# Waiting inside TensorE's own queue where the fill banks change rows, and one dealing of the fills for all slots

## The chip, the cores and the metric

The kernel runs on one core of one Trainium2 chip. A core has five engines that run side by side, each through its own queue in order: TensorE (PE in the profile; its weight loads are listed apart as PEld), VectorE (DVE), ScalarE (ACT), GpSimd (POOL) and SyncE (SP), which issues the transfers. Engines wait for each other through semaphores. The metric is the device time of one execution in microseconds (us). Time before: 720.57 us, the median of 3 runs (719.08 to 722.27).

## What is computed

The input has 2048 tokens of 512 channels. Sliding-window attention with 32 heads of 16 channels (window 256) gives `s`; a channel MLP gives a gate; all is float32.

```python
def reference(A_x, A_wqkv, A_wo, B_x, B_w1, B_b1, B_w2, B_b2):
    x = A_x                                  # (1, 2048, 512)
    xn = _layernorm(x)
    s = _A_ref(xn, A_wqkv, A_wo)             # q, k, v = xn @ wqkv; 32 heads of 16; 0 <= i - j < 256
                                             # softmax(q k^T / 4) v @ wo
    g = _silu(_B_ref(xn, B_w1, B_b1, B_w2, B_b2))
                                             # gelu(layernorm(xn) @ w1 + b1) @ w2 + b2, hidden size 1792
    return x + s * g
```

## The kernel before

**Stages.** First the tokens are normalised and transposed and the first projections are made (steps t = -16 to -1). Then the attention runs over 64 *slot pairs* u = 0 to 63 (128 slots, t = 2u and 2u + 1): eight groups of four heads, and in each group eight pairs of query blocks. From some 403 us on come the MLP, the output projection and the end.

**Fills.** Everything that attention doesn't need at once (the projections of later head groups, the values, and the first hidden rows of the MLP) is cut into single pairs of matmuls, the *fills*, and these are put between the attention's own matmuls. A fill pair uses the array by halves: one matmul on the upper 64 rows of the array, one on the lower 64, side by side, each into a PSUM bank of its own (`fb0`, `fb1`; in the first stage also the banks named `pair`). A job goes through two phases. In phase 0 bank 0 gets the products of one half of the rows and bank 1 those of the other; in phase 1 the banks change rows, so that each bank ends with a whole sum. [...] That is the *turn* of a job. `tandem` (line 505) makes two jobs of 12 pairs (24 for the values) a phase over a span of slots (t0, t1), mostly six slots long; `by_halves` (line 360) does it for the first stage.

**How a turn is secured.** An otherwise useless small write of another engine stands between: it waits for the last pair of phase 0, and the first pair of phase 1 waits for it. This *mark* is a VectorE memset of one column (`fixed[:, 7:8]`), a ScalarE copy or a GpSimd memset, and it stands in that engine's queue between its other work. Where no mark is named, `by_halves` lets the turn wait for VectorE's last masked copy of the attention maxima (`outs["max"]`).

**How the slots are dealt.** A slot pair's work on TensorE is set by the loop at lines 991 to 1034: scores of the exponentials (`prob_part`, into `stb`, read by ScalarE), products for the row maxima (`max_ends` into `xy`, `max_middle` into `zo`, read by VectorE), fills, and the product with the values (`pv_part`, into `zo`, named `zo<-pt,vt` in the profile). `some(todo, first, last)` issues the quarters `first` to `last` of a slot's fills. An ordinary even slot issues one quarter, then the products of `max_middle`, then the other three; an ordinary odd slot issues `early` quarters, `max_middle`, then up to `last`, `max_ends`, and the rest. For spans of six slots (`turned`, all but the spans of the values' later jobs and the last one) the slot t0 + 2 is in `turns`: there all fills of phase 0 are issued ahead of `max_middle`, and in the odd slot after it `early` and `last` are one to two quarters later.

**Order on an engine.** The class `Ordered` keeps each engine's instructions in the order of the program text; no scheduler moves them.

Of the kernel before, what the change touches and what calls it, by code (L numbers as in the profile page):

```python
# [23 lines left out]
NQ = H // 4  # L24
EPS = 1e-5
LEAD = 12
EARLY = 10
ORDER = mybir.DependencyInfo(mybir.DependencyClass.Sync, mybir.DependencyReason.DATA)
# [21 lines left out]
def mixer_kernel(ctx, tc, x, wqk, wv, wo, w1, b1, w2, b2, out):  # L50


    nc = SimpleNamespace(**{name: Ordered(tc, name) for name in ("tensor", "vector", "scalar", "gpsimd", "sync")})
# [131 lines left out]
    ends_of = xy.rearrange("q a (p e k) -> q a p e k", p=2, e=2)  # L185
    psf = attn.enter_context(tc.tile_pool(name="psf", bufs=1, space=PSUM))
    fb = [psf.tile([P, 512], F32, name=f"fb{i}") for i in range(2)]
    early = ExitStack()
# [27 lines left out]
    fixed = const.tile([P, 8], F32, name="fixed")  # L216
    mhalf = fixed[:, 0:4]
# [7 lines left out]
    mask = upper.bitcast(I32).unsqueeze(1).unsqueeze(1).to_broadcast([P, 2, 2, P])  # L225
    b1s = const.tile([P, NF], F32, name="b1s")
    sv = small.tile([P, 32], F32, tag="sv", name="sv", bufs=1)
# [129 lines left out]
            return half, finish, box  # L357
        return [(216, mm, i) for i in range(len(ops))], finish

    def by_halves(job, banks, first, second, seer=None):  # L360

        half, finish, box = job
        box[:] = banks
        seen = []
        for phase, where in enumerate((first, second)):
            for i in range(12):
                flags = dict(start=(phase == 0 and i == 0), stop=(phase == 1 and i == 11), skip_group_check=True)

                def unit(i=i, phase=phase, flags=flags):
                    if phase == 0 and i == 0:  # L370
                        box[:] = [bank() if callable(bank) else bank for bank in box]
                    two = (half(box[1 - phase], 1 - phase, i, slice(64, P), **flags),
                           half(box[phase], phase, i, slice(0, 64), **flags))
                    if phase == 0 and i == 11 and seer:
                        seen.append(seer())
                        for r in two:
                            tc.add_manual_dep(seen[0].ins, r.ins.name, ORDER, reason="the rows are through")
                    if phase == 1 and i == 0:
                        for r in two:
                            tc.add_manual_dep(r.ins, (seen or outs["max"])[0].ins.name, ORDER, reason="the banks change rows")  # L380
                fills.setdefault(where[len(where) * i // 12], []).append((unit, ()))
        fills[second[-1]].append((finish, ()))

# [76 lines left out]
        return t  # L460

    taken = set()
    turns = set()
    todo_dve = []

    def late(fn, *args):
# [38 lines left out]
    def tandem(t0, t1, one, two, mid=None, back=None):  # L505

        n = one[0]
        lo, hi, seen = slice(0, 64), slice(64, P), []
        turned = t1 - t0 == 5 and not back
        mid = mid or (t0 + t1 + 1) // 2  # L510

        def places(slots):
            cuts = [n * k // len(slots) for k in range(len(slots) + 1)]
            return [(t, 0) for t, a, b in zip(slots, cuts, cuts[1:]) for _ in range(b - a)]
        if turned:
            turns.add(t0 + 2)
        first, second = places(range(t0, mid)), places(range(back or mid, t1 + 1))
        for phase, where in enumerate((first, second)):
            for i in range(n):
                flags = dict(start=(phase == 0 and i == 0), stop=(phase == 1 and i == n - 1), skip_group_check=True)  # L520

                def unit(i=i, phase=phase, flags=flags):
                    made = ((two if phase == 0 else one)[1](fb[1 - phase], i, hi, **flags),
                            (one if phase == 0 else two)[1](fb[phase], i, lo, **flags))
                    if phase == 0 and i == n - 1:
                        seen.append(nc.scalar.copy(fixed[:, 6:7], mhalf[:, 0:1]) if t0 < 16 * NQ - LEAD and not turned else
                                    nc.vector.memset(fixed[:, 7:8], 0.0))
                        for r in made:
                            tc.add_manual_dep(seen[0].ins, r.ins.name, ORDER, reason="the rows are through")
                    if phase == 1 and i == 0:  # L530
                        for r in made:
                            tc.add_manual_dep(r.ins, seen[0].ins.name, ORDER, reason="the banks change rows")
                fills.setdefault(where[i], []).append((unit, ()))
        fills.setdefault((t1, 0), []).append((one[2], (fb[0], t1, nc.scalar.copy)))
        if t1 >= 16 * NQ - LEAD:
            fills[t1, 0].append((two[2], (fb[1], t1, nc.vector.tensor_copy)))
        else:
            fills.setdefault((t1, 2), []).append((two[2], (fb[1], t1, nc.scalar.copy)))
# [27 lines left out]
    def max_ends(n, qb):  # L566

        mt, _ = max_places(n, qb)
        for p in range(2):
            for a in (1, 0):  # L570
                if qb == 0:
                    max_scores(ends_of[:, a, p, 0], n, qb, a, p, lambda row: row[:, P * qb: P * qb + 1].to_broadcast([64, P]))
                    max_scores(ends_of[:, a, p, 1], n, qb, a, p, lambda row: row[:, P * qb: P * (qb + 1)])
                else:
                    max_scores(ends_of[:, a, p], n, qb, a, p,
                               lambda row: row.rearrange("d (b k) -> d b k", k=P)[:, max(qb - 2, 0): qb + 1: 2 if qb > 1 else 1])
        own = ends_of[:, :, :, 1]
        outs["max"] = nc.vector.copy_predicated(own, mask, ends_of[:, :, :, 0]),
        return lambda: nc.vector.tensor_reduce(out=mt, in_=own, axis=AX.X, op=ALU.max, negate=True)

    def max_middle(n, qb):
# [259 lines left out]
    def free_bank():  # L841
        return ps_st.tile([P, 512], F32, tag="b", name=f"pair_{now[0]}")

    others = [free_bank, free_bank]
    by_pool, by_dve, by_act = (lambda: nc.gpsimd.memset(sv[:, 31:32], 0.0), lambda: nc.vector.memset(sv[:, 30:31], 0.0),
                               lambda: nc.scalar.copy(sv[:, 29:30], mhalf[:, 0:1]))
    for job, banks, first, second, *seer in (
            (job_qk(0, 2), fb, [(-8, 0)], [(-7, 0)]), (job_v(0, 4), others, [(-8, 0), (-8, 1)], [(-7, 1)], by_dve),
            (job_v(0, 5), fb, [(-5, 0)], [(-5, 1)], by_act), (job_qk(0, 3), others, [(-5, 1)], [(-4, 1)], by_pool),
            (job_v(0, 6), fb, [(-4, 0)], [(-4, 1), (-3, 1)]), (job_v(0, 7), fb, [(-2, 1), (-1, 1)], [(-1, 2)], by_pool),  # L850
            (job_qk(1, 0), others, [(-3, 1)], [(-2, 1)]),
            (job_qk(1, 1), fb, [(0, 0)], [(1, 0)], by_act)):
        by_halves(job, banks, first, second, *seer)
    fills.update(spread([job_x(3)], [(-6, 0), (-6, 1)]))
    fills[-10, 0][:0] = fills[-11, 1][-5:]
    del fills[-11, 1][-5:]
# [129 lines left out]
    def some(todo, first, last):  # L986

        n = sum(fn.__name__ == "unit" for fn, _ in todo)
        for fn, args in todo[-(-n * first // 4): -(-n * last // 4) if last < 4 else len(todo)]:
            fn(*args)  # L990
    for u in range(end // 2):
        t = 2 * u
        prob_part(u, 1)
        rest = own_max(max_ends, t + LEAD)
        calm[0] = t < end - LEAD
        even, odd = (fills.pop((v, 0), []) for v in (t, t + 1))
        now[:] = t, 0
        run(delayed.pop((t, 0), ()))
        early = 4 if t in turns else 1
        some(even, 0, early)  # L1000
        own_max(max_middle, t + LEAD)
        rest()
        planned(t)
        some(even, early, 4)
        fill_in(t, 1)
        ended(t)
        t += 1
        prob_part(u, 2)
        now[:] = t, 0
        run(delayed.pop((t, 0), ()))  # L1010
        early = 2 if u % 8 == 7 else 1
        last = 2 if u % 8 == 0 else 3
        if t - 1 in turns:
            early, last = last, last + 1
        some(odd, 0, early)
        own_max(max_middle, t + LEAD)
        some(odd, early, last)
        planned(t)
        fill_in(t, 1)
        own_max(max_ends, t + LEAD)()  # L1020
        calm[0] = False
        own_rows(t + LEAD, t)
        for fn, args in todo_dve:
            fn(*args)
        todo_dve.clear()
        if u % 8:
            some(odd, last, 4)
        if t + 1 < end:
            prob_part(u + 1, 0)
        if u % 8 == 0:  # L1030
            some(odd, last, 4)
        fill_in(t, 2)
        pv_part(u)
        ended(t)
# [483 lines left out]
```

## Time and profile before

| what | value |
|---|---|
| median of 3 runs | 720.57 us (719.08 to 722.27) |
| the profiled execution's own time | 720.63 us |
| span of the profile | 718.5 us |
| PE busy | 709.2 us (99%) |
| DVE, ACT, POOL busy | 507.9, 409.5, 298.4 us (71, 57, 42%) |
| granted TensorE clock | 0.999 |
| VectorE marks in tile `fixed` | 19, 59 ns each, first at 75.5, last at 394.2 us |
| ScalarE marks in `fixed` and `sv` | 3 of 191 ns, 2 of 192 ns |

Times in the windows and rows are counted from the span's start. A slot pair is measured here from the start of its predecessor's product with the values to the start of its own. Matmuls are pipelined and their ends are modelled, so a busy PE isn't PE at its peak: a stall shows as a later start. In a row of the timeline x8 is a run of eight matmuls, and the time beside the start goes from the first one's start to the last one's end.

### The profile page before, as it was taken

To read this page: it belongs to the slowest core of one execution; us is meant where nothing else is said; L and a number is where in the kernel's file an instruction comes from. 1 tells how busy PE (TensorE), PEld (TensorE's weight loads), DVE (VectorE), ACT (ScalarE), POOL (GpSimd) and SP (SyncE) were. 2 spreads that over 40 slices of the span, in tenths; PEclk is the share of its full clock that TensorE was granted. 3 is DMA by queue.
4 is the path that set the end of the run, shared out by engine and by line. 5 is a ranking of instruction groups with operands and counts; after the bars stand their busy time and mean duration, and the time that the engine had idled before them with its cause. 6 is when DMAs were issued, how large, how long until landed. Compare 5 with 4: busy or idle time off the path is not lost.

```text
span 718.5 us, 17700 instructions
## 1 busy us (share of the span) xinstructions
PE 709.2 (99%) x6912; PEld 573.6 (80%) x6912; DVE 507.9 (71%) x880; ACT 409.5 (57%) x612; POOL 298.4 (42%) x498
## 2 busy tenths in 40 slices
PE   8999999999999999999999999999999999999997
PEld 7998777777778887767777788888888888888886
DVE  6887778878777677788893767346586856767923
ACT  7767777767676676768877735132354644541001
POOL 7344767666576655757777340204203000001102
PEclk9999999999999999999999999999999999999999
DMA  8325366776448876677744658155222312253701
GB/s 298 84 49 117 89 150 147 174 185 140 94 101 255 271 261 199 176 179 201 201 135 136 200 170 290 66 149 202 88 88 89 118 58 88 82 186 120 243 15 59
DMA packets 66274, 106.95 MB, mean 149 GB/s; under 512 B 12624, under 2 KB 21072, under 8 KB 66192
## 3 DMA queue, kind: packets, MB, share of 16 engines
q1 hardware_dynamic: 66192, 105.82, 51.1%
q8 instruction: 55, 0.90, 0.5%
q14 instruction: 27, 0.22, 0.1%
HBM read 54.80 MB, written 33.82 MB: 123 GB/s over the span
## 4 chain that ended last, share of the span: by engine, by line
PE 93%; DVE 2%; ACT 2%; DMA 1%; POOL 1%; issue 1%; SPq 0%; DVEq 0%; ACTq 0%; POOLq 0%
PE acc L42 21%; PE fb L42 21%; PE zo L42 15%; PE p L42 9%; PE stb L42 7%; PE s L42 6%; PE h L42 6%; PE xy L42 6%; PE pv L42 2%; ACT pt L42 1%; DVE mt L42 1%; DMA x<-in_x_dram 1%; DMA w<-w_d 0%; DVE xy L42 0%; PE tr L42 0%
## 5 line engine op out<-in xcount | busy, mean ns | idle before, releaser
L42 ACT ACTIVATE pt<-stb 128x1024 f32<-128x1024 f32 (+1 forms) x176 | 177.6, 1009 | 49.6 <-PE stb L42 42.5
L42 POOL TENSOR_SCALAR_AFFINE_SELECT pt<-pt 128x512 f32<-128x512 f32 (+1 forms) x296 | 163.7, 573 | 73.7 <-ACT pt L42 70.1
L42 DVE COPY_PREDICATED xy<-upper,xy 128x512 f32<-128x512 int32 x128 | 88.9, 694 | 37.2 <-PE xy L42 34.9
L42 PE MATMUL fb<-xnT,wqb 64*128 64x512 f32 (+2 forms) x732 | 114.0, 390 | 0.5 <-DVE xy L42 0.2
L42 POOL TENSOR_TENSOR xo<-xo,gated 128x512 f32<-128x512 f32 x15 | 19.9, 1329 | 221.5 <-DVE gated L42 220.5
L42 PE MATMUL acc<-w,gh 128*128 128x512 f32 x320 | 98.6, 389 | 0.0
L42 PE MATMUL zo<-pt,vt 128*17 128x128 f32 (+1 forms) x1920 | 90.5, 327 | 0.8 <-DVE mt L42 0.6
L42 DVE TENSOR_REDUCE mt<-xy 128x4 f32<-128x512 f32 x128 | 88.0, 688 | 2.9 <-DVE xy L42 0.6
L42 DVE TENSOR_REDUCE mt<-zo 128x4 f32<-128x512 f32 x120 | 82.8, 690 | 9.8 <-PE zo L42 7.5
L42 PE MATMUL stb<-qk 64*128 64x384 f32 (+1 forms) x704 | 77.8, 298 | 1.5 <-ACT pt L42 1.0
L42 PEld LDWEIGHTS zo<-pt,vt 128*17 128x17 f32 x1920 | 50.3, 97 | 33.5 <-POOL pjr L42 2.6
L42 PEld LDWEIGHTS stb<-qk 64*128 64x128 f32 x704 | 54.9, 185 | 22.3 <-ACT pt L42 12.5
L42 PEld LDWEIGHTS acc<-w,gh 128*128 128x128 f32 x320 | 60.1, 188 | 12.5
L42 PEld LDWEIGHTS fb<-xnT,wqb 64*128 64x128 f32 (+1 forms) x732 | 62.4, 186 | 5.3 <-DVE fixed L42 0.5
L42 PE MATMUL acc<-w,gl 128*128 128x512 f32 x160 | 62.3, 389 | 0.0
L42 PE MATMUL xy<-qk 64*128 64x256 f32 (+2 forms) x576 | 62.2, 298 | 0.0
L42 PEld LDWEIGHTS xy<-qk 64*128 64x128 f32 x576 | 45.3, 186 | 8.7 <-DVE mt L42 4.2
L42 PE MATMUL p<-xnT 128*128 128x512 f32 x189 | 51.8, 389 | 0.0
L42 PEld LDWEIGHTS zo<-qk 64*128 64x128 f32 x480 | 39.7, 185 | 10.7 <-DVE mt L42 6.4
L42 PE MATMUL s<-wos,ohl 128*128 128x512 f32 (+1 forms) x204 | 44.3, 377 | 0.0
L42 ACT ACTIVATE gated<-acc 128x512 f32<-128x512 f32 x16 | 8.7, 596 | 61.9 <-DVE acc L42 61.9
L42 PE MATMUL zo<-qk 64*128 64x128 f32 x480 | 43.4, 258 | 0.3
(208 smaller groups left out, 1217.5 us busy)
## 6 DMA issues: line engine op xcount, KB each, us to landing
qk<-sh SPq DMA_DIRECT2D x128, 128.0 KB
qk<-pjr SPq DMA_DIRECT2D x64, 128.0 KB
oT_d<-oraw SPq DMA_DIRECT2D x64, 128.0 KB
w_d<-in_w_dram SPq DMA_DIRECT2D x14, 512.0 KB
xt_d<-xnT SPq DMA_DIRECT2D x12, 512.0 KB
x<-in_x_dram SPq DMA_DIRECT2D x16, 256.0 KB
w<-w_d SPq DMA_DIRECT2D x16, 256.0 KB
or<-oT_d SPq DMA_DIRECT2D x16, 256.0 KB
```

What stands on the lines that cost most here:

```text
L42: r = issue(*args, **kwargs)
```

## The change

Four edits go together.

1. Where a job turns, `rows_change` issues an empty instruction of TensorE's own queue that waits for the last two matmuls of phase 0. It stands right ahead of the first fill of phase 1.
2. The marks go: 20 memsets on VectorE, 5 copies on ScalarE and 2 memsets on GpSimd, with the choice between them. The turns that waited for VectorE's masked copy now wait for phase 0 too.
3. `turns` and `turned` go. The slots t0 + 2 and t0 + 3 are dealt as all others.
4. Nothing else: the same matmuls, copies and transfers are issued.

```diff
+    def rows_change(seen):
+
+        gate = nc.tensor.nop()
+        for r in seen:
+            tc.add_manual_dep(gate.ins, r.ins.name, ORDER, reason="a bank changes rows")
...
-    def by_halves(job, banks, first, second, seer=None):
+    def by_halves(job, banks, first, second):
...
+                    if phase == 1 and i == 0:
+                        rows_change(seen)
                     two = (half(box[1 - phase], 1 - phase, i, slice(64, P), **flags),
                            half(box[phase], phase, i, slice(0, 64), **flags))
-                    if phase == 0 and i == 11 and seer:
-                        seen.append(seer())
-                        for r in two:
-                            tc.add_manual_dep(seen[0].ins, r.ins.name, ORDER, reason="the rows are through")
-                    if phase == 1 and i == 0:
-                        for r in two:
-                            tc.add_manual_dep(r.ins, (seen or outs["max"])[0].ins.name, ORDER, reason="the banks change rows")
+                    if phase == 0 and i == 11:
+                        seen.extend(two)
...
-        turned = t1 - t0 == 5 and not back
...
-        if turned:
-            turns.add(t0 + 2)
...
+                    if phase == 1 and i == 0:
+                        rows_change(seen)
                     made = ((two if phase == 0 else one)[1](fb[1 - phase], i, hi, **flags),
                             (one if phase == 0 else two)[1](fb[phase], i, lo, **flags))
                     if phase == 0 and i == n - 1:
-                        seen.append(nc.scalar.copy(fixed[:, 6:7], mhalf[:, 0:1]) if t0 < 16 * NQ - LEAD and not turned else
-                                    nc.vector.memset(fixed[:, 7:8], 0.0))
-                        for r in made:
-                            tc.add_manual_dep(seen[0].ins, r.ins.name, ORDER, reason="the rows are through")
-                    if phase == 1 and i == 0:
-                        for r in made:
-                            tc.add_manual_dep(r.ins, seen[0].ins.name, ORDER, reason="the banks change rows")
+                        seen.extend(made)
...
-        early = 4 if t in turns else 1
-        some(even, 0, early)
+        some(even, 0, 1)
         own_max(max_middle, t + LEAD)
         rest()
         planned(t)
-        some(even, early, 4)
+        some(even, 1, 4)
...
-        if t - 1 in turns:
-            early, last = last, last + 1
```

**TensorE in slot pair 5** (t = 10 and 11, the middle of the span (8, 13)), before, from the last of the even slot's eight fills (`fb`) on: `zo<-qk` are the products of `max_middle`, `stb` the scores for the second exponential. The names in brackets are the queues whose semaphores a row waits for.

```order
L42 MATMUL fb_111<-xnT,wqb_1389 128x512
L42 MATMUL zo<-qk_763 128x128 [waits Activation_49]
L42 MATMUL zo<-qk_763 128x128 x3
L42 MATMUL stb<-qk_94 128x256 [waits Activation_49]
L42 MATMUL stb<-qk_94 128x256 x3
L42 MATMUL fb_111<-xnT,wqb_1389 128x512 [waits DVE_49]
L42 MATMUL fb_112<-xnT,wqb_1389 128x512
L42 MATMUL fb_111<-xnT,wqb_1389 128x512
L42 MATMUL fb_112<-xnT,wqb_1389 128x512
L42 MATMUL fb_111<-xnT,wqb_1389 128x512
L42 MATMUL fb_112<-xnT,wqb_1389 128x512
L42 MATMUL zo<-qk_763 128x128 [waits DVE_49]
```

The same place with the change, from the even slot's `max_middle` on, behind its first two fills:

```order
L42 MATMUL zo<-qk_764 128x128 [waits Activation_49]
L42 MATMUL zo<-qk_764 128x128 x3
L42 MATMUL fb_112<-xnT,wqb_1390 128x512
L42 MATMUL fb_111<-xnT,wqb_1390 128x512
L42 MATMUL fb_112<-xnT,wqb_1390 128x512
L42 MATMUL fb_111<-xnT,wqb_1390 128x512
L42 MATMUL fb_112<-xnT,wqb_1390 128x512
L42 MATMUL fb_111<-xnT,wqb_1390 128x512
L42 MATMUL stb<-qk_94 128x256 [waits Activation_49]
L42 MATMUL stb<-qk_94 128x256 x3
L42 MATMUL fb_111<-xnT,wqb_1390 128x512 [waits PE_49]
L42 MATMUL fb_112<-xnT,wqb_1390 128x512
```

The four matmuls of the even slot's `max_middle` stand six fills earlier. Only the four score matmuls are left between the end of phase 0 and the turn, where eight matmuls stood. The odd slot's `max_middle` follows two fills behind the turn, and not six. No instruction is added to TensorE's queue: the empty instruction's wait stands at the first fill of phase 1.

**TensorE in slot pair 23** (t = 46 and 47, the last one of a head group, which has no third block of scores), with the change:

```order
L42 MATMUL fb_112<-xnT,wqb_2915 128x512
L42 MATMUL fb_111<-xnT,wqb_2915 128x512
L42 MATMUL fb_111<-xnT,wqb_2915 128x512 [waits PE_49]
L42 MATMUL fb_112<-xnT,wqb_2915 128x512
L42 MATMUL fb_111<-xnT,wqb_2915 128x512
L42 MATMUL fb_112<-xnT,wqb_2915 128x512
L42 MATMUL zo<-qk_764 128x128 [waits DVE_49]
```

Here nothing is left between the last fill of phase 0 and the turn; before, the four `zo<-qk` of the even slot stood there. Slot pair 47 reads the same.

**TensorE in the first stage**, the turn of the job `job_qk(0, 2)`, as a piece of the difference (`pair` are the fills of the job that runs beside it):

```order
 L42 MATMUL pair_-8_609<-wva,xnT 128x256
 L42 MATMUL pair_-8_608<-wva,xnT 128x256
-L42 MATMUL fb_111<-xnT,wqb_221 128x256 [waits DVE_49]
+L42 MATMUL fb_111<-xnT,wqb_221 128x256 [waits PE_49]
 L42 MATMUL fb_112<-xnT,wqb_221 128x256
 L42 MATMUL fb_111<-xnT,wqb_221 128x256
```

The turn stands where it stood, and waits for TensorE's matmuls of phase 0 instead of VectorE's queue.

More of the change, by code (lines that the diff above doesn't have):

```diff
@@ L462, in mixer_kernel @@
     taken = set()
-    turns = set()
     todo_dve = []
@@ L577, in max_ends @@
         own = ends_of[:, :, :, 1]
-        outs["max"] = nc.vector.copy_predicated(own, mask, ends_of[:, :, :, 0]),
+        nc.vector.copy_predicated(own, mask, ends_of[:, :, :, 0])
         return lambda: nc.vector.tensor_reduce(out=mt, in_=own, axis=AX.X, op=ALU.max, negate=True)
@@ L844, in mixer_kernel @@
     others = [free_bank, free_bank]
[L845 to L850, printed above, removed]
+    for job, banks, first, second in (
+            (job_qk(0, 2), fb, [(-8, 0)], [(-7, 0)]), (job_v(0, 4), others, [(-8, 0), (-8, 1)], [(-7, 1)]),
+            (job_v(0, 5), fb, [(-5, 0)], [(-5, 1)]), (job_qk(0, 3), others, [(-5, 1)], [(-4, 1)]),
+            (job_v(0, 6), fb, [(-4, 0)], [(-4, 1), (-3, 1)]), (job_v(0, 7), fb, [(-2, 1), (-1, 1)], [(-1, 2)]),
             (job_qk(1, 0), others, [(-3, 1)], [(-2, 1)]),
-            (job_qk(1, 1), fb, [(0, 0)], [(1, 0)], by_act)):
-        by_halves(job, banks, first, second, *seer)
+            (job_qk(1, 1), fb, [(0, 0)], [(1, 0)])):
+        by_halves(job, banks, first, second)
     fills.update(spread([job_x(3)], [(-6, 0), (-6, 1)]))
```

## The prediction

> **What bounds the kernel now.** First the page: its head and the chain that ended last.
>
> ```profile
> span 718.5 us, 17700 instructions
> PE 709.2 (99%) x6912; PEld 573.6 (80%) x6912; DVE 507.9 (71%) x880; ACT 409.5 (57%) x612; POOL 298.4 (42%) x498
> PE 93%; DVE 2%; ACT 2%; DMA 1%; POOL 1%; issue 1%; SPq 0%; DVEq 0%; ACTq 0%; POOLq 0%
> ```
>
> TensorE carries the chain, so only what lets its matmuls start earlier counts. A busy PE hides small stalls; so I measured the slot pairs by windows, each from the start of one product with the values to the start of the next. A sum row has the length of all windows, the busy time of each engine, and the means of a window. First the eight pairs with a turn inside a head group whose even slot has a `max_middle` (u = 5, 11, 14, 20, 29, 38, 44, 53), then 13 pairs of the same kind without one (3, 4, 6, 21, 22, 27, 28, 30, 37, 46, 51, 52, 54).
>
> ```profile
> sum 43.97, PE 43.89 PEld 32.83 DVE 33.82 ACT 32.13 POOL 35.47; mean PE 5.49 PEld 4.10 DVE 4.23 ACT 4.02 POOL 4.43
> sum 67.60, PE 67.60 PEld 53.90 DVE 55.96 ACT 52.88 POOL 44.74; mean PE 5.20 PEld 4.15 DVE 4.30 ACT 4.07 POOL 3.44
> ```
>
> 43.97 / 8 = 5.50 us with a turn, 67.60 / 13 = 5.20 us without, with the same load on ACT (means 4.02 and 4.07) and DVE (4.23 and 4.30): 0.30 us a turn. The same for the second pair of a group (u = 2, 26, 50 with a turn; 10, 18, 42 without) and the last one (23, 47 with; 7, 15, 39, 55 without):
>
> ```profile
> sum 16.91, PE 16.33 PEld 12.23 DVE 11.12 ACT 12.85 POOL 13.69; mean PE 5.44 PEld 4.08 DVE 3.71 ACT 4.28 POOL 4.56
> sum 15.78, PE 15.70 PEld 12.29 DVE 12.21 ACT 11.93 POOL 10.42; mean PE 5.23 PEld 4.10 DVE 4.07 ACT 3.98 POOL 3.47
> sum 10.87, PE 10.84 PEld 7.59 DVE 8.88 ACT 5.02 POOL 5.37; mean PE 5.42 PEld 3.80 DVE 4.44 ACT 2.51 POOL 2.68
> sum 20.19, PE 20.19 PEld 15.05 DVE 17.73 ACT 11.37 POOL 10.25; mean PE 5.05 PEld 3.76 DVE 4.43 ACT 2.84 POOL 2.56
> ```
>
> 5.64 against 5.26, and 5.44 against 5.05: 0.38 us each. In the first pair of a group a turn costs nothing: 5.73 us in pair 56 with one, 5.72 in pair 24 without.
>
> ```profile
> 365.58:371.31 5.73, 5.62 (x81) 3.97 (x77) 4.47 (x10) 4.12 (x6) 3.29 (x8) 1.00 0.10 30
> 189.58:195.30 5.72, 5.65 (x79) 4.05 (x77) 5.02 (x10) 4.36 (x6) 4.03 (x8) 1.00 0.37 92
> ```
>
> Where the 0.30 us go, the timeline tells. An ordinary pair (u = 3), then the turn in u = 5:
>
> ```profile
> 79.77 0.40 PE L42 MATMUL fb<-xnT,wqb 64*128 64x512 f32 x2
> 80.00 0.33 PE L42 MATMUL zo<-qk 64*128 64x128 f32 x4
> 80.17 0.91 PE L42 MATMUL fb<-xnT,wqb 64*128 64x512 f32 x6
> 80.58 0.69 DVE L42 TENSOR_REDUCE mt<-zo 128x4 f32<-128x512 f32 x1
> 80.91 0.42 PE L42 MATMUL stb<-qk 64*128 64x256 f32 x4
> 81.05 0.19 PEld L42 LDWEIGHTS fb<-xnT,wqb 64*128 64x128 f32 x2
> 81.17 0.40 PE L42 MATMUL fb<-xnT,wqb 64*128 64x512 f32 x2
> ```
>
> ```profile
> 90.20 1.09 PE L42 MATMUL fb<-xnT,wqb 64*128 64x512 f32 x8
> 91.13 0.33 PE L42 MATMUL zo<-qk 64*128 64x128 f32 x4
> 91.37 0.06 DVE L42 MEMSET fixed<- 128x1 f32 x1 [0.27 <-PE fb L42]
> 91.57 0.69 DVE L42 TENSOR_REDUCE mt<-zo 128x4 f32<-128x512 f32 x1
> 92.32 0.30 PEld L42 LDWEIGHTS zo<-qk 64*128 64x128 f32 x4 [0.30 <-DVE mt L42]
> 92.92 0.30 PEld L42 LDWEIGHTS xy<-qk 64*128 64x128 f32 x4 [0.19 <-DVE mt L42]
> ```
>
> In the ordinary pair the first `zo` products come 0.23 us behind the slot's first fill, and VectorE's maximum of them starts 0.81 us behind that fill. In the turn they come behind all eight fills, 0.93 us, and the maximum 1.37 us. The odd slot's `zo` products, which must not overwrite what is being read, then wait for VectorE, and so do the `xy` products behind them. Over the whole kernel such waits add up to
>
> ```profile
> PEld zo L42 <- DVE mt L42: 6.4, 21, 0.5
> PEld xy L42 <- DVE mt L42: 4.2, 22, 0.2
> ```
>
> 10.6 us of idle weight loads, part of it under matmuls in flight. In the ordinary pair no such wait stands: TensorE's own work bounds it.
>
> **The change, part by part.**
>
> *Dealing.* With it the order in the turned pairs is the ordinary one, so their waits should go: 8 x 0.30 = 2.4, 3 x 0.38 = 1.1, 2 x 0.38 = 0.8, together 4.3 us. The bounds: nothing, if something that I don't see makes these pairs long; 4.3 us, if all of it is the dealing. I take all, since DVE, ACT and PEld do no more work in them than in their twins.
>
> *The wait itself.* It adds no instruction, but the turn moves close behind phase 0 and holds back a weight load that ran ahead so far. In the ordinary pair the six fills end at 80.17 + 0.91 = 81.08, and the load for the next fill, behind four score matmuls as at the new turns, starts at 81.05: 0.03 us before that end. What the wait makes of it no row shows. The nearest is a turn with a VectorE mark in the same place:
>
> ```profile
> 74.29 1.16 PE L42 MATMUL fb<-xnT,wqb 64*128 64x512 f32 x8
> 75.28 0.41 PE L42 MATMUL stb<-qk 64*128 64x256 f32 x4
> 75.52 0.06 DVE L42 MEMSET fixed<- 128x1 f32 x1
> 75.64 0.53 PEld L42 LDWEIGHTS fb<-xnT,wqb 64*128 64x128 f32 x6 [0.15 <-DVE fixed L42]
> ```
>
> The fills end at 75.45, the mark starts 0.07 later, ends at 75.58, and the load goes 0.06 after that: end plus 0.19. Without the mark one step of 0.06 to 0.07 is left: end plus 0.07, against end minus 0.03: 0.10 us late. Bounds: 0, if the signal is there before the load would go; 0.22 (0.19 + 0.03), if a wait for one's own matmuls is no shorter than the way through VectorE. I take 0.10. Behind the held load stands TensorE's whole queue, and these pairs are bounded by it, so each counts: 11 x 0.10 = 1.1 us. Pairs 23 and 47 have nothing between. From the run of eight, 1.09 us, less the 0.40 that a lone pair is in flight, pairs follow each other every (1.09 - 0.40) / 3 = 0.23 us. The next pair would start 0.17 before the end, and its load leads it by 0.12 (81.05 to 81.17): at end minus 0.29. With the wait it goes at end plus 0.07, 0.36 late: 2 x 0.36 = 0.7 us. Turns in the first two pairs of a group (8, 56, 17, 41) gain nothing from the dealing and may lose 0.10 each; half of that may hide under ACT's exponentials: 0.2 us. The three turns of the values' later jobs have a whole product with the values between and cost nothing; the one in pair 59 keeps four products between, as before, and is about even.
>
> [...]
>
> *Marks.* 20 memsets of 59 ns, 5 copies of 0.19 us and 2 memsets of 0.10 leave DVE, ACT and POOL. In the slots none is on the path by its own length: the wait for DVE is for the maxima. In the first stage three turns lie on the path:
>
> ```profile
> 38.48 0.65 PEld L42 LDWEIGHTS fb<-xnT,wqb 64*128 64x128 f32 x10 [0.43 <-DVE xy L42]
> ...
> 60.49 0.10 POOL L42 MEMSET sv<- 128x1 f32 x1 [4.67 <-PE fb L42]
> 60.64 0.53 PEld L42 LDWEIGHTS fb<-wva,xnT 64*128 64x128 f32 x8 [0.25 <-POOL sv L42]
> ...
> 64.91 0.19 ACT L42 COPY sv<-fixed 128x1 f32<-128x1 f32 x1 [1.24 <-PE fb L42]
> 65.16 0.41 PEld L42 LDWEIGHTS fb<-xnT,wqb 64*128 64x128 f32 x6 [0.26 <-ACT sv L42]
> ...
> 40.00:50.00 10.00, 10.00 (x148) 9.45 (x146) 8.32 (x13) 6.35 (x14) 5.90 (x9) 1.00 0.39 83
> ```
>
> At 38.48 phase 0 was long through (its last `fb` pair lies before the whole `pair` phase): the wait of 0.43 goes, say 0.4. At 60.64 the load comes 0.15 us behind the start of the mark, at 65.16 0.25: a direct wait leaves out the mark and one of the two steps, 0.2 us on the mean. Together 0.8 us. TensorE is busy throughout in the window between the first and the second of these turns, so I count all; at the least none of it counts.
>
> *Sum.* -4.3 + 1.1 + 0.7 + 0.2 - 0.8 = -3.1 us. Span 718.5 to 715.4; the execution's own time 720.63 to 717.5. The median of the runs shown, 720.57, is the same within 0.1, so I predict 717.5 us, -0.43%.
>
> **The rivals.**
>
> *A: the wait is met when it is reached.* All 4.3 and 0.8 come, and only pairs 23 and 47 pay half: -4.8, 715.8 us. For it: 0.10 is little, and ACT's exponential sometimes holds the score matmuls a little, which covers the load. Against: the load at 81.05 runs before the end of the fills, so a wait for that end can't be free.
>
> *B: the wait costs as much as the mark did.* 0.22 in place of 0.10: 11 x 0.12 + 2 x 0.12 + 0.2 = 1.8 us worse: -1.3, 719.3 us. [...]
>
> *C: the turned pairs aren't long through the dealing.* Then 4.3 stays away, and with 2.0 of waits against 0.8: +1.2, 721.8 us. For it: in the first pair of a group a turn costs nothing, so the dealing doesn't always bind. Against: the two waits for DVE that the ordinary pair doesn't have.
>
> *D, the other side: the gated load must wait until the score matmuls between are through as well, and TensorE starts anew.* In the ordinary pair they end at 80.91 + 0.42 = 81.33; plus 0.07 is 81.40, 0.35 after 81.05. Thirteen turns x 0.35 = 4.6, and 0.35 in each of pairs 8, 56, 17 and 41 and of the two later first-stage turns, 2.1: 6.7 against 4.3 and the 0.4 of the first turn: +2.0, 722.6 us. It decides from 4.7 / 19 = 0.25 us a turn on. Against: at 75.64 a turn is through while its score matmuls, 75.28 + 0.41 = 75.69, aren't.
>
> That the change doesn't do what it says is unlikely: the order shows the wait at each turn's first fill, and no mark.
>
> **How the numbers follow.** The forecast 0.52, A 0.20, B 0.13, C 0.09, D 0.06. About 0.5%, 3.6 us, is what a measurement can tell from no change; the border lies at 717.0. Two fifths of the forecast (0.20) and nearly all of A (0.18) lie below it: faster 0.38. Of C and D 0.04 lie above 724.2. The rest, 0.58, is within 0.5%. The range goes from A less the spread of runs to between B and C: 715.0 to 720.4.
>
> **What would show it.** The windows of the turned pairs at 5.3 (u = 5 and its like), 5.35 (u = 2) and 5.4 (u = 23), with the maximum of `zo` some 0.8 us behind the slot's first fill. The waits PEld zo and xy for DVE mt at 5 us or less in all. The load at a turn some 0.07 us behind the end of the fills of phase 0. The first stage 0.8 us shorter. Wrong, if the turned pairs stay at 5.5 us (C), if the load at a turn comes 0.2 us or more behind the end of the fills (B, D), or if they come out at 5.2 (A).

## The result, and the profile after

The changed kernel takes 715.23 us (median of 6 runs, 714.12 to 717.40) beside 722.09 us for the kernel before (6 runs, 719.08 to 722.58): a ratio of the means of 0.9919, 95% interval 0.9896 to 0.9942. Run again on two later occasions it gave 0.9930 (0.9906 to 0.9954) and 0.9908 (0.9885 to 0.9931). So the change makes the kernel 0.7 to 0.9% faster, 5 to 7 us. The time lies inside the predicted range, 0.23 us from its lower end, but the gain is nearly twice the 0.43% of the forecast. On the second occasion the executions with a mean granted clock below 0.999 were 2.2 us (before) and 2.5 us (changed) longer than the others, and the two kernels lie 5.3 us apart among the ones and 5.6 us among the others.

The head of the page and the chain that ended last, after:

```profile
span 713.3 us, 17671 instructions
PE 704.3 (99%) x6912; PEld 572.9 (80%) x6912; DVE 508.3 (71%) x860; ACT 408.2 (57%) x607; POOL 297.5 (42%) x496
PE 94%; ACT 2%; DMA 1%; POOL 1%; DVE 1%; issue 1%; ACTq 0%; POOLq 0%; DVEq 0%
```

The same matmuls; DVE has 20 instructions less, ACT 5 and POOL 2: the marks. TensorE carries the chain as before. In all kernels run here the first fill pair of phase 1 is kept behind the last pair of phase 0 at a turn, by a mark, by VectorE's masked copy or by a wait of TensorE's own; what becomes of the sums without that order no run shows.

The slot pairs by windows, sum rows as in the prediction. First the kernel before: the turned pairs 5, 11, 14, 20, 29 and 38 (44 and 53 are left out here: both lie in a stretch in which transfers disturb, see below), and the turned pairs 17 and 41.

```profile
sum 32.97, PE 32.89 PEld 24.73 DVE 24.87 ACT 23.72 POOL 26.02; mean PE 5.48 PEld 4.12 DVE 4.15 ACT 3.95 POOL 4.34
sum 9.69, PE 9.69 PEld 7.16 DVE 6.51 ACT 7.60 POOL 7.25; mean PE 4.84 PEld 3.58 DVE 3.26 ACT 3.80 POOL 3.62
```

After, the same two groups, then 2, 26 and 50, and last 23 and 47:

```profile
sum 31.46, PE 31.46 PEld 25.12 DVE 25.58 ACT 23.72 POOL 24.45; mean PE 5.24 PEld 4.19 DVE 4.26 ACT 3.95 POOL 4.08
sum 9.23, PE 9.23 PEld 7.49 DVE 6.74 ACT 7.61 POOL 6.78; mean PE 4.62 PEld 3.74 DVE 3.37 ACT 3.81 POOL 3.39
sum 15.68, PE 15.68 PEld 12.23 DVE 11.70 ACT 12.39 POOL 12.70; mean PE 5.23 PEld 4.08 DVE 3.90 ACT 4.13 POOL 4.23
sum 10.38, PE 10.25 PEld 7.38 DVE 8.75 ACT 5.01 POOL 5.43; mean PE 5.13 PEld 3.69 DVE 4.37 ACT 2.51 POOL 2.72
```

A turned pair now takes 31.46 / 6 = 5.24 us (5.50 before), one of the second kind 5.23 (5.64), one of the third 5.19 (5.44), and pairs 17 and 41 take 4.61 (4.85). The ordinary pairs without a turn stay at 5.2 us.

Pair 5 in the timeline after, from the slot's first fill on:

```profile
87.89 0.40 PE L42 MATMUL fb<-xnT,wqb 64*128 64x512 f32 x2
88.12 0.33 PE L42 MATMUL zo<-qk 64*128 64x128 f32 x4
88.29 0.90 PE L42 MATMUL fb<-xnT,wqb 64*128 64x512 f32 x6
88.70 0.69 DVE L42 TENSOR_REDUCE mt<-zo 128x4 f32<-128x512 f32 x1
89.03 0.41 PE L42 MATMUL stb<-qk 64*128 64x256 f32 x4
89.26 0.19 PEld L42 LDWEIGHTS fb<-xnT,wqb 64*128 64x128 f32 x2
89.29 0.47 PE L42 MATMUL fb<-xnT,wqb 64*128 64x512 f32 x2
```

The maximum starts 88.70 - 87.89 = 0.81 us behind the first fill (1.37 before). Phase 0 ends at 88.29 + 0.90 = 89.19. The load of the turn starts at 89.26, 0.07 us later, while the score matmuls between, 89.03 + 0.41 = 89.44, are still running. The waits over the whole kernel, after:

```profile
PEld xy L42 <- DVE mt L42: 1.9, 10, 0.2
PEld zo L42 <- DVE mt L42: 1.5, 7, 0.3
PEld fb L42 <- PE fb L42: 1.0, 2, 0.5
```

The first two held 10.6 us before and hold 3.4 now. The third is new: 0.5 us each at the two turns with nothing between, pairs 23 and 47.

**Where the time went.** I add the lengths by stretches, from the profiled execution of before and from three of the changed kernel (the first one, and those of the two later occasions):

| stretch | before | changed, three executions |
|---|---|---|
| start to the first product with the values | 67.54 | 65.64, 66.45, 65.72 |
| pairs 1 to 43 | 232.97 | 229.44, 229.24, 229.59 |
| pairs 44 to 54 | 60.02 | 60.57, 61.37, 58.48 |
| pairs 55 to 63 | 40.91 | 40.66, 40.71, 40.65 |
| all that follows | 317.09 | 316.99, 317.03, 317.03 |
| span | 718.5 | 713.3, 714.8, 711.5 |

Pairs 1 to 43 give 3.4 to 3.7 us, every time. The start gives 1.1 to 1.9 us, of which 0.7 is the change (below) and the rest the first loads: before, VectorE stood 0.99 us waiting for the third load of `x` (at 6.59), in the first execution of the changed kernel it didn't, and the first projection starts at 11.09 and at 9.94 us. Between the three executions of the changed kernel the start varies by 0.81 us. The stretch 44 to 54 varies by 2.9 us between executions of one and the same kernel; there ScalarE waits for transfers.

### The profile page after: what moved, and what is told of

It is laid out like the page before. It is cut to its first block, busy times and chain, and to the rows that moved or that the text cites. A ratio compares the mean times of both kernels' runs of the same rounds, so it can differ in the third digit from the quotient of the medians.

```text
span 713.3 us, 17671 instructions
## 1 busy us (share of the span) xinstructions
PE 704.3 (99%) x6912; PEld 572.9 (80%) x6912; DVE 508.3 (71%) x860; ACT 408.2 (57%) x607; POOL 297.5 (42%) x496
## 4 chain that ended last, share of the span: by engine, by line
PE 94%; ACT 2%; DMA 1%; POOL 1%; DVE 1%; issue 1%; ACTq 0%; POOLq 0%; DVEq 0%
PE acc L42 21%; PE fb L42 21%; PE zo L42 15%; PE p L42 9%; PE stb L42 7%; PE s L42 6%; PE h L42 6%; PE xy L42 5%; PE pv L42 2%; ACT pt L42 1%; DMA w<-w_d 1%; POOL pt L42 0%; DMA x<-in_x_dram 0%; PE tr L42 0%; DVE mt L42 0%
## 5 line engine op out<-in xcount | busy, mean ns | idle before, releaser
L42 PE MATMUL fb<-xnT,wqb 64*128 64x512 f32 (+2 forms) x732 | 119.2, 393 | 0.3
L42 PE MATMUL fb<-xnT 64*128 64x512 f32 (+1 forms) x240 | 44.0, 404 | 0.1
```

Source lines behind the costliest of these rows:

```text
L42: r = issue(*args, **kwargs)
```

## Experiments

The pair lengths of the first four runs stand in one table, in us (means of the windows of a kind; in brackets stands the number of the run). The eleven ordinary pairs are the 13 of the prediction without 28 and 46, which were longer in single executions of the changed kernel (5.40 and 6.47 us).

| pairs | before | changed | old dealing, wait (2) | new dealing, marks (1) | waits behind scores (3) | waits with nothing between (4) |
|---|---|---|---|---|---|---|
| 5, 11, 14, 20, 29, 38 | 5.50 | 5.24 | 5.50 | 6.03 | 5.24 | 5.58 |
| 2, 26, 50 | 5.64 | 5.23 | 5.50 | 5.80 | 5.22 | 5.57 |
| 23, 47 | 5.44 | 5.19 | 5.43 | 5.99 | 5.19 | 5.53 |
| 17, 41 | 4.85 | 4.61 | 4.85 | 5.41 | 4.61 | 4.94 |
| eleven ordinary ones | 5.20 | 5.19 | 5.20 | 5.19 | 5.25 | 5.50 |
| 7, 15, 39, 55 (last of a group) | 5.04 | 5.05 | 5.04 | 5.05 | 5.18 | 5.21 |

**1. The new dealing with the old marks.** The kernel before, and only the extra quarters go:

```diff
-        if turned:
-            turns.add(t0 + 2)
```

> The kernel before with one edit: all slots are dealt alike, the marks of VectorE and ScalarE stay. Theory (the dealing was held back by the marks: a mark stands in VectorE's queue behind the maxima, and dealing alike puts two of them, which end some 4.1 us into the pair, ahead of it): the turn's load goes at about 4.2 us in place of 3.4, the turned pairs come to 5.9 to 6.0 us (5.50 before, 5.24 changed), the whole to about 5 us over the kernel before. Rival (the dealing gains by itself, whoever marks the turn): turned pairs 5.3, some 4 us under the kernel before.

Measured: 726.36 us, 1.0071 of before (1.0051 to 1.0091), so 5 to 6 us slower. The timeline in pair 5:

```profile
89.76 0.91 PE L42 MATMUL fb<-xnT,wqb 64*128 64x512 f32 x6
90.16 0.69 DVE L42 TENSOR_REDUCE mt<-zo 128x4 f32<-128x512 f32 x1
90.77 0.68 DVE L42 TENSOR_REDUCE mt<-xy 128x4 f32<-128x512 f32 x1
91.40 0.06 DVE L42 MEMSET fixed<- 128x1 f32 x1
91.53 0.19 PEld L42 LDWEIGHTS fb<-xnT,wqb 64*128 64x128 f32 x2 [0.82 <-DVE fixed L42]
```

A line of its waits, and the sum row of the six turned pairs:

```profile
PEld fb L42 <- DVE fixed L42: 14.3, 18, 1.3
```

```profile
sum 36.19, PE 32.51 PEld 24.79 DVE 25.51 ACT 23.74 POOL 28.31; mean PE 5.42 PEld 4.13 DVE 4.25 ACT 3.96 POOL 4.72
```

Phase 0 is through at 90.67, but the mark is written at 91.40: in VectorE's queue two maxima of 0.69 and 0.68 us stand ahead of it. The old dealing was what kept the turn away from those maxima. Beside the changed kernel's 5.24 us it cost 0.26 a pair, and spared 0.79. Here the new dealing is worth something only with the wait.

**2. The old dealing with the wait.** The changed kernel, with the extra quarters put back:

```diff
+        if t1 - t0 == 5 and not back:
+            turns.add(t0 + 2)
...
+        early = 4 if t in turns else 1
-        some(even, 0, 1)
+        some(even, 0, early)
...
-        some(even, 1, 4)
+        some(even, early, 4)
...
+        if t - 1 in turns:
+            early, last = last, last + 1
```

> The changed kernel with the old dealing of the turned slots put back; TensorE's own waits and no marks. Theory (the pairs gain through the dealing): the eight turned pairs stay at 5.45 to 5.50 us, pairs 2, 26 and 50 at 5.55; the first stage is 0.8 us shorter; in all 1 to 1.5 us under the kernel before. Rival (it is the marks in the queues that cost, and the dealing is indifferent): turned pairs 5.2 to 5.3, some 5 us under the kernel before.

Measured: 717.25 us, 0.9954 (0.9937 to 0.9971). The sum rows of the six turned pairs and of 17 and 41:

```profile
sum 32.98, PE 32.89 PEld 24.76 DVE 24.69 ACT 23.75 POOL 26.08; mean PE 5.48 PEld 4.13 DVE 4.12 ACT 3.96 POOL 4.35
sum 9.69, PE 9.69 PEld 7.15 DVE 6.38 ACT 7.61 POOL 7.25; mean PE 4.84 PEld 3.58 DVE 3.19 ACT 3.81 POOL 3.63
```

They are as long as before to 0.01 us. So the length of these pairs is the dealing, as the theory says, and rival C falls. In the table the wait alone gains only in 2, 26 and 50 (0.14 us each). The time fell by 3.4 us, more than the 1 to 1.5 expected; the trace shows 2.3 us of span, 1.6 of them ahead of the first product with the values, where the first loads vary. What the other executions gained beyond that isn't shown.

**3. More waits, behind score matmuls.** The changed kernel with the same wait at the odd slot's first fill in nearly all other pairs:

```diff
+    recent = []
...
+                    recent[:] = made
...
+        if recent and odd:
+            rows_change(recent)
```

> The changed kernel with a needless wait of the same kind ahead of the first fill of every odd slot, for the last fill pair ahead of it: 38 more with four score matmuls between and 6 more with nothing between. Theory (0.10 us a wait behind score matmuls, 0.36 without): the ordinary pairs go from 5.15-5.20 to 5.25-5.30, in all 38 x 0.10 + 6 x 0.36 = 6.0 us over the changed kernel, a fifth less where a pair has slack. Rival A (met when reached): under 1 us. Rival B (0.22 each): 38 x 0.22 + 6 x 0.48 = 11 us. Rival D (0.35 each): 15 us.

Measured: 717.76 us, 0.9952 (0.9935 to 0.9969), 2.4 us above the changed kernel's 0.9919; by the trace 2.9 us over the slot pairs without the disturbed ones, about half of the 6.0 expected. The load at a wait comes 0.055 to 0.064 us behind the modelled end of the last fill, at all 53 places with a whole pair of 512 columns; rival B's 0.19 occurs nowhere. But an ordinary pair only grows from 5.19 to 5.25 us, the sum row of the eleven:

```profile
sum 57.78, PE 57.78 PEld 46.25 DVE 47.54 ACT 44.32 POOL 38.91; mean PE 5.25 PEld 4.20 DVE 4.32 ACT 4.03 POOL 3.54
```

That is less than the 0.10 that the load is late. Where the rest goes the rows of pair 3 show, first in the kernel before, without a wait, then in this run:

```profile
80.91 0.42 PE L42 MATMUL stb<-qk 64*128 64x256 f32 x4
81.17 0.40 PE L42 MATMUL fb<-xnT,wqb 64*128 64x512 f32 x2
81.40 0.36 PE L42 MATMUL zo<-qk 64*128 64x128 f32 x4
81.60 0.68 PE L42 MATMUL fb<-xnT,wqb 64*128 64x512 f32 x4
```

```profile
78.91 0.42 PE L42 MATMUL stb<-qk 64*128 64x256 f32 x4
79.14 0.19 PEld L42 LDWEIGHTS fb<-xnT,wqb 64*128 64x128 f32 x2
79.17 0.47 PE L42 MATMUL fb<-xnT,wqb 64*128 64x512 f32 x2
79.47 0.34 PE L42 MATMUL zo<-qk 64*128 64x128 f32 x4
79.64 0.68 PE L42 MATMUL fb<-xnT,wqb 64*128 64x512 f32 x4
```

The held fill itself starts 0.26 us behind the scores in both. The products behind it come 0.30 us after it in place of 0.23, and the next fills 0.47 in place of 0.43: of the 0.07 us, 0.03 are made up.

With nothing between, pairs 7, 15, 39 and 55 grow by 0.14 us, but pairs 31 and 63, which also end their group, by 0.32 and 0.33.

**4. Waits with nothing between.** The changed kernel with a wait between two fill pairs in the even slot:

```diff
+    recent = []
...
+                    recent[:] = made
...
-        some(even, 1, 4)
+        some(even, 1, 2)
+        if recent and even:
+            rows_change(recent)
+        some(even, 2, 4)
```

> The changed kernel with about 60 further empty waits for TensorE's own last fill pair, directly ahead of the next fill pair, in the even slots: nothing stands between the waiting and the awaited pair. By my prediction (0.36 us each, as worked out for pairs 23 and 47): 60 x 0.36 = 22 us over the changed kernel, the ordinary pair at 5.55 us. By what the waits ahead of score matmuls showed where the attention leaves slack (0.13 to 0.14 each): 8 us, the ordinary pair at 5.33 us. By a wait that is met when it is reached: below 1 us. If a wait with nothing between lets the array run empty and start anew (0.6 us each or more): 36 us or more, the ordinary pair at 5.8 us.

Measured: 731.42 us, 1.0146 (1.0122 to 1.0169). That is 15 us above the changed kernel beside it (716.44). A line of its waits, and the sum row of the eleven ordinary pairs:

```profile
PEld fb L42 <- PE fb L42: 24.2, 63, 0.5
```

```profile
sum 60.51, PE 59.82 PEld 45.37 DVE 47.57 ACT 44.29 POOL 37.56; mean PE 5.44 PEld 4.12 DVE 4.32 ACT 4.03 POOL 3.41
```

24.2 / 63 = 0.38 us of idle weight loads for a wait, and 60.51 / 11 - 5.19 = 0.31 us of pair length. That is near my 0.36. But in pairs 7, 15, 39 and 55 it is 0.16, about what run 3 had shown there. Neither expectation fits all pairs. Nor is it the place in the group: pairs 23 and 47 are the last of theirs too, have the wait of their turn already, and grow by 0.34 us with this second one. That looks as if these pairs had some 0.2 us to spare, which a first wait uses up; what it is these runs don't show.

**5. The first stage's marks put back.** The changed kernel with the marks and the masked copy in `by_halves`, as in the kernel before:

```diff
-    def by_halves(job, banks, first, second):
+    def by_halves(job, banks, first, second, seer=None):
...
-                    if phase == 1 and i == 0:
-                        rows_change(seen)
...
+                    if phase == 0 and i == 11 and seer:
+                        seen.append(seer())
```

> The changed kernel, but the turns of the first stage are secured by the marks of VectorE, ScalarE and GpSimd again, and by VectorE's masked copy; the slots stay as changed. Theory (the first stage gained 0.7 to 0.8 us): 0.7 us over the changed kernel (ratio to before about 0.993), the three turns at 0.39, 0.21 and 0.21 us later than with the wait, and all slot pairs as in the changed kernel to 0.03 us. Rival (TensorE's first stage is held by something else, so that what the turns gain is lost again by the first slot): the same time as the changed kernel.

Measured: 716.31 us, 0.9941 (0.9919 to 0.9963), beside 716.44 for the changed kernel: the time can't tell 0.7 us. The trace can. The timeline at the first turn, with the marks:

```profile
38.16 1.50 PEld L42 LDWEIGHTS fb<-xnT,wqb 64*128 64x128 f32 x24 [0.41 <-DVE xy L42]
```

and in the changed kernel:

```profile
36.86 1.51 PEld L42 LDWEIGHTS fb<-xnT,wqb 64*128 64x128 f32 x24
```

The wait of 0.41 us is gone. Against the changed kernel's execution of the last occasion the starts of the same matmuls fall back by 0.40, 0.20 and 0.20 us at the three turns, 0.74 in all by the end of the stage.

**6. Pair 45.** After the change this pair is longer, 7.76 us in place of 6.51. ScalarE's row there, changed kernel:

```profile
306.48 0.62 ACT L42 CAST w<-w 128x512 fp32r<-128x512 f32 x1 [2.69 <-DMA w<-w_d]
```

A cast of the MLP's weights stands in ScalarE's queue ahead of an exponential and waits 2.69 us for its transfer. I moved the cast one slot pair later, and measured that on two occasions:

```diff
-    for f, t, lo_at, lo_by in ((6, 90, 93, nc.vector), ...
+    for f, t, lo_at, lo_by in ((6, 92, 93, nc.vector), ...
```

> The changed kernel with ScalarE's cast of the first MLP weights moved from step 90 to step 92. Theory (in the changed kernel pair 45 is 7.76 us long, since ScalarE stands at this cast until the weights' transfer lands, 2.7 us, where it stood 1.4 us before the change; the exponential behind it is late, and TensorE with it): pair 45 comes to 5.2 us, 2.0 to 2.5 us under the changed kernel. Rival (the transfer is late for the next user too, or the path has its slack elsewhere): under 0.5 us.

> The changed kernel with ScalarE's cast of the third part of the MLP's first weights one slot pair later, as tried before. If the cast costs the changed kernel 1.4 to 2.6 us at pair 45 in every execution: 0.989 of before, 2 us below the changed kernel run beside it. If the late transfer is chance, or the time is lost elsewhere: the same as the changed kernel within 1 us.

Measured: 0.9915 (0.9890 to 0.9940) and 0.9919 (0.9894 to 0.9944); beside the second the changed kernel itself had 0.9930 (0.9906 to 0.9954). No difference that can be told. Pair 45 is 5.19 and 5.18 us, as the theory said, but pair 53 is 8.67 and 9.11 in place of 5.24. A stall moved.

The changed kernel itself, beside the second:

> The changed kernel itself once more, beside the others on one chip. If the late transfer ahead of pair 45 belongs to the kernel, pair 45 is again 6.5 us or longer; if it is chance of one execution, it may be as short as 5.2 us. Time: 0.992 of before, as measured already.

Pair 45 was 7.50 us again, and pair 46 6.47, since the granted clock dropped to 0.50 there, from 308.0 to 311.3 us (see the last section).

**7. The transfer earlier.** In the changed kernel and in the one before, the transfer goes one slot earlier into SyncE's queue:

```diff
-    for f, t in ((6, 87), (7, 92), ...
+    for f, t in ((6, 86), (7, 92), ...
```

> The changed kernel with one transfer (w<-w_d, the third part of the MLP's first weights that is loaded, 128x512) one slot earlier in SyncE's queue: ahead of one oT_d, one 16 KB and six qk transfers instead of behind them; ScalarE's cast stays where it was. Theory (ScalarE's cast waits 2 to 3 us for this transfer since TensorE comes to it earlier than before, and so gives back about 1.2 us of the gain): pair 45 at 5.2 to 5.3 us in place of 7.5 to 7.8, no new stall, 2 us below the changed kernel: ratio to before 0.989 to 0.990. Rival (the transfers as a whole are the limit there, so that a stall only moves to another one): pair 45 short, another pair longer by 1.5 us or more, ratio as in the changed kernel, 0.992 to 0.993.

> The kernel before with the same transfer one slot earlier. Theory: pair 45 at 5.2 us in place of 6.5, ratio 0.998; the gap to the changed kernel with the same edit is then 1.0% (7 us: 4.4 in the slots, 0.7 in the first stage, and the rest of pairs 9, 43 and the like), larger than that between before and changed. Rival: a stall only moves: ratio 1.000 within 0.002.

Measured: 0.9932 (0.9908 to 0.9956) and 0.9974 (0.9959 to 0.9989). In both traces pair 45 is short (5.19, 5.20) and pair 53 long (9.64, 8.13 us), as the rival said. The gap between the two kernels, expected at 1.0%, is only 0.42%. In the traces pair 53 is 1.5 us longer in the changed kernel; how much of the missing gap that explains over all executions isn't shown. ScalarE in pair 53, changed kernel with the early transfer:

```profile
348.13 0.37 ACT L42 COPY oraw<-zo 128x256 f32<-128x256 f32 x1 [3.53 <-DMA oT_d<-oraw]
```

In the kernel before the edit gains 0.26%, though its profiled execution shows the new stall: that one took 722.03 us, the median of the runs is 719.30. One trace is not what every execution does.

**8. Transfers spread.** On top of the early transfer, the five last loads of these weights go one to two slots later:

```diff
-                 (13, 100), (2, 100), (3, 102), (0, 102), (1, 104), (4, 104), (5, 106)):
+                 (13, 100), (2, 100), (3, 104), (0, 104), (1, 105), (4, 106), (5, 108)):
```

> The changed kernel with the transfer ahead of pair 45 one slot earlier, as tried, and the five last loads of the MLP's first weights (xnT<-w_d and w<-w_d) one to two slots later each; two of them then stand behind the oT_d transfer that ScalarE waited for in pair 53, instead of ahead of it. If SyncE's order alone makes that wait: pair 45 at 5.2, pair 53 1.1 us or more shorter than the 9.6 with the early transfer alone (two issues of 0.54 us each and what they take of the engines), no other pair longer than 0.3 us; at the best 5.3, and the kernel then 2.4 us below the changed one, 0.989 to 0.990 of before. If the volume of transfers in this stretch is the limit, the stretch from pair 44 to 54 takes 60.5 us or more again, and the ratio is 0.992 to 0.993.

> The changed kernel once more, beside the one with the spread transfers: pair 45 at 7.5 to 7.8, pair 53 at 5.3, the stretch from pair 44 to 54 at 60.5 to 61.4 us, ratio 0.992 to 0.993.

Measured: 713.88 us, 0.9895 (0.9874 to 0.9916), beside 714.15, 0.9908 (0.9885 to 0.9931). It is the lowest ratio of all, but the two can't be told apart. Pair 45 is 5.21 and 53 is 5.26; now 44 is 6.62, and the stretch from 44 to 54 takes 59.19 us, so neither expectation holds as a whole. And the changed kernel missed its expectation: pair 45 took 5.45 and the stretch 58.48, without any edit. That stretch in the windows, first before, then after, then the changed kernel's last execution:

```profile
300.51:360.53 60.02, 58.63 (x820) 43.91 (x816) 49.51 (x87) 47.16 (x66) 41.31 (x73) 1.00 0.71 182
```

```profile
295.08:355.64 60.56, 57.89 (x820) 43.67 (x816) 49.08 (x83) 47.04 (x66) 41.45 (x74) 1.00 0.71 184
```

```profile
295.31:353.79 58.48, 57.89 (x820) 43.61 (x816) 49.10 (x83) 47.06 (x66) 41.49 (x74) 1.00 0.73 188
```

PE is busy for the same 57.89 us in both executions of the changed kernel; what differs, 2.1 us, is TensorE standing still. So the late transfer is not a fixed cost of the change. Which transfer comes late differs between kernels and between executions. Whether their order or their volume decides stays open.

## Why the prediction was right, and where it was off

The mechanism was right: the dealing lengthened the turned pairs, and a wait in TensorE's own queue lets it go at a small price. That the time lies inside the range is in part luck. It does so by 0.23 us, beside a kernel before that measured 722.09 us and not the 720.57 from which the prediction counted; on the last occasion the changed kernel took 714.15 us, which is outside. The gain was forecast too small: the waits were priced too high, and gains in pairs that it held to be indifferent were left out.

**The dealing, -4.3 us: right.** Runs 1 and 2 show that the dealing makes these pairs long, and that it can go only with the wait. Pairs 5 to 38 gained 0.26 net; if the wait costs there the 0.06 that it costs an ordinary pair, that is 0.32 for the dealing, where the prediction had 0.30. Pairs 23 and 47 gained 0.25, with the 0.14 that the wait costs in pairs 7, 15, 39 and 55 that is 0.39, where it had 0.38. In 2, 26 and 50 the gain was 0.41, of which run 2 gives 0.14 to the wait in place of the mark: with the old dealing their mark cost something by itself, which the prediction denied.

**The wait, 11 x 0.10 = 1.1 us: the lateness right, the price too high.** The load comes some 0.06 us behind the modelled end, near the 0.07 worked out. The 53 waits of run 3 lie at 0.055 to 0.064 us. But the step "these pairs are bounded by it, so each counts" failed: a load that is 0.10 us later doesn't make its own fill start later, the products behind it come 0.07 us late, and 0.03 of that is made up (the rows of pair 3 in run 3). A pair grows by 0.06 (run 3), 11 of them by 0.7 us and not 1.1.

**Pairs 23 and 47, 2 x 0.36 = 0.7 us: the worst sized term.** The lateness is real: 0.38 us a wait in run 4, 0.31 of it on the path in an ordinary pair. But a first wait in a pair of this kind costs only 0.14 to 0.16 (7, 15, 39, 55 in runs 3 and 4), and pairs 23 and 47 come out 0.14 above these. The prediction took the bound of one kind of pair for another; 0.3 us, not 0.7.

**Pairs 8, 56, 17 and 41, +0.2 us: wrong for 17 and 41.** "Turns in the first two pairs of a group gain nothing" rested on pair 56 beside 24, the first of a group. For the second of a group it shows no row. Its twins without a turn, 9, 25 and 49, were no shorter than 17 and 41 in the kernel before (4.95 to 4.97 against 4.85), and yet 17 and 41 gained 0.24 each, by run 2 through the dealing: a twin that is no shorter didn't prove that the place costs nothing. Pair 56 is unchanged (5.73), as predicted; pair 8 lost 0.22, by run 2 through the dealing too (5.72 there).

**Left out: pairs 12, 18, 43 and 57, which have no turn, and 59.** They got 0.19, 0.14, 0.22, 0.11 and 0.12 us shorter, 0.8 in all; the prediction counted gains only in the turned pairs, and held the turn in 59 to be even. In run 2, with the old dealing, 18, 43 and 59 were short already (5.16, 5.19, 4.33), so there it is the wait in place of the mark; 12 wasn't (5.48, but 5.30 in run 1), so there it is the dealing; 57 became short with both only. What holds these pairs in the kernel before I haven't shown.

**The first stage, -0.8 us: right,** 0.74 by run 5.

**The rivals.** B falls by the 0.055 to 0.064. D falls too: the load at 89.26 goes while the score matmuls run to 89.44. C falls by run 2. A came closest, 715.8 us, since it had the waits nearly free. The sign that the prediction set for it, turned pairs at 5.2 us and not at 5.3, came nearly true: they are at 5.24, 5.23 and 5.19. But its mechanism is wrong: the wait is not met when it is reached, since the load is late at every place, and run 3 shows a price.

**The sum.** Pairs 1 to 43 were predicted at 6 x 0.20 + 2 x 0.28 + 0.02 less 0.15 = 1.6 us and gave 3.5. The difference is made of 17 and 41 (0.57, with the loss that was predicted), 12, 18 and 43 (0.55), 5 to 38 (0.3), 2 and 26 (0.25), 23 (0.2), less 0.2 in pair 8 and 0.1 in pair 28. The last 0.24 are pair 9, and not the change: 4.95 us in the traced execution of the kernel before, 4.69 in the one with the early transfer. Pairs 44 to 54 were predicted at 0.7 and gave between -1.4 and +1.5, with the transfers; 55 to 63 were predicted even and gave 0.2. By runs, outside pairs 44 to 54, the wait in place of the marks, with the old dealing, gave 1.6 us in the trace of run 2 (0.74 in the first stage, 0.8 in pairs 2, 18, 26, 43 and 59), where the prediction had 0.8; the new dealing on top of it gave 2.7, where the prediction had 1.6 with its waits.

## What to carry to other kernels

Count a mark on another engine with the queue that it stands in, not with its own 0.06 us: here two maxima ahead of it made a turn 0.8 us late, and the order of the work had been bent, at 0.26 us a pair, to avoid that. In these runs a wait for TensorE's own matmuls held the next load until 0.06 us behind their end; it cost 0.06 us of pair length where score matmuls stood between, and 0.3 directly between two fill pairs (0.14 to 0.16 in pairs that seem to have time to spare). Before pricing a place by a twin, ask whether the twin has the same time to spare, and don't take a twin that is no shorter as proof that a place is free.

## What the runs showed of the hardware

A stall of TensorE can cost twice. The windows of the changed kernel with the early transfer, 1 us each, in the stall of pair 53 and behind it (columns: length, busy time of PE, PEld, DVE, ACT and POOL with the number of instructions, granted clock, DMA share, GB/s):

```profile
347.00:348.00 1.00, 0.00 (x0) 0.00 (x0) 0.00 (x0) 0.00 (x0) 0.00 (x0) 1.00 1.02 347
348.00:349.00 1.00, 0.44 (x6) 0.44 (x8) 0.00 (x0) 0.87 (x2) 0.00 (x0) 1.00 1.12 307
349.00:350.00 1.00, 1.00 (x10) 0.78 (x10) 0.89 (x2) 0.94 (x2) 0.50 (x1) 0.76 0.85 244
350.00:351.00 1.00, 1.00 (x12) 0.91 (x10) 0.40 (x1) 0.68 (x1) 1.00 (x3) 0.50 0.93 338
351.00:352.00 1.00, 1.00 (x9) 0.81 (x9) 0.69 (x1) 0.85 (x2) 1.00 (x2) 0.50 0.63 168
352.00:353.00 1.00, 1.00 (x10) 0.88 (x8) 0.55 (x1) 0.00 (x0) 0.34 (x1) 0.53 0.83 293
353.00:354.00 1.00, 1.00 (x27) 0.60 (x27) 0.93 (x3) 0.78 (x1) 0.00 (x0) 1.00 0.12 33
```

TensorE stood still for 2.64 us, went on at 348.56 at full clock, and was then granted half of it: 0.24 + 0.50 + 0.50 + 0.47 = 1.7 us are lost, which is 3.4 us at half speed, on top of the stall. The same drop, some 3.4 us long, follows gaps of 1.23, 1.48, 1.69, 1.82 and 2.12 us in other executions; it does not follow gaps of 1.04, 1.12, 1.69, 2.19 and 2.30 us. So the length of the gap alone does not decide; what else does, these runs don't show. One drop is a mean clock lower by 1.7 / 715 = 0.0024, as in the executions at 0.997 and 0.998.
